# A new order for 1,400 steps: attention with a small state, fused with a snake MLP, on one core

## The chip, the core and the metric

The kernel runs on one core of one Trainium2 chip. A core has five engines with their own instruction queues: TensorE (PE; its weight loads, PEld, are listed apart), VectorE (DVE), ScalarE (ACT), GpSimd (POOL) and SyncE (SP). Sixteen DMA engines move data between the chip's main memory and the core; here SP, ACT and POOL issue transfers. Matmul results are in PSUM, which has eight banks. Each engine does its instructions in order and waits on semaphores for the others.

The metric is the device time of the kernel in microseconds (us). Before the change it is 221.43, the median of three runs (221.27 to 221.89).

## The reference: what is computed

```python
B, H, S, Ns, D = 8, 8, 512, 32, 64
scores = x @ state^T / sqrt(D)          # x: B H S D, state: B H Ns D
xread  = softmax(scores) @ state        # B H S D
scores2 = state @ x^T / sqrt(D)
sread  = softmax(scores2) @ x           # B H Ns D
y = concat([xread, sread], axis=2)      # to rows (B * 544) x 512
h = y @ w_in                            # 512 x 2048
g = h + sin(alpha * h)**2 / (alpha + 1e-9)
out = g @ w_out                         # 2048 x 512, out is 4352 x 512, float32
```

## The kernel before

The product with w_in is moved ahead of the attention's second matmul: for each batch the kernel forms M = state @ w_in once (step `m`), and then h = A @ M, where A holds the softmax weights. So each batch b = 0 to 7 is one tile t of 512 tokens, and the 256 state rows of all batches (32 each) form a ninth tile, t = 8. All matmuls are bf16, accumulated in float32.

There is no loop. The list `ORDER` (from line 21) names every step, with its arguments, in the order in which the program is written; `Steps` has one method for each name, and the last lines run them (lines 629 to 633). Since each engine works in order, this list sets the order of every engine and of every DMA queue. The framework adds the semaphores. Letters A, V, G in a step's arguments put it on ACT, DVE or POOL; a number behind the tile's indices is a PSUM bank, which can be taken only when what was in it has been read.

For a batch b the steps are, in the order in which they depend on each other:

- `lx.b` (line 271): POOL issues the load of x, cast to bf16, into `xnat` (three buffers). Batch 0 comes through `lq`, four float32 loads on SP.
- `pk.b.part` (344): DVE brings half of the heads into the layout `xp`, in which pairs of heads lie side by side. `xq` does it for batch 0.
- `td.b` (387): a DMA transpose, issued by SP, makes `xT` out of `xp`, for batches 2 to 7. Batches 0 and 1 are transposed on TensorE instead (`xtq` 358, `xt` 371) and copied out of PSUM (`xc` 382).
- `sc.b.g` (394): scores for half of the heads; `ex` exponentials on ACT; `rs` and `rr` the row sums and their reciprocals on DVE; `nm` (418) the normalised weights A; `ad.b` (438) a DMA transpose of A into `AT`, issued by SP (batch 0: `at` and `ac`, through TensorE).
- `m.b.s` (478): slice s (512 columns) of M for both halves g, eight matmuls of 64 x 32 weights, which run beside each other in parts of the array; `me` (495) copies a half out of its bank.
- `w`, `cs`, `rc`, `xs` (445 to 474): the second softmax, whose result goes into `xs_all` for tile 8.

For each tile t and each of the sixteen blocks f of 128 hidden columns: `h.t.f` (531) is two matmuls of 512 columns (`hg`, line 549, is one of the two; for t = 8, four of 256); `si` (557) the sine on ACT, `sq` (564) its square on ACT, DVE or POOL, `gt` (573) the sum g on DVE, which frees the bank of h. Then `o.t.st.f0.f1` (581) adds blocks f0 to f1 − 1 into output rows st; `oc` (592) copies the finished bank to `o_sb` (six buffers) on ACT or DVE, and `os` (597) stores it, issued by SP. Tile 7's rows st = 3 are done in two pieces, `oh`, `och`, `osh`, of 384 and 128 columns. The stores of tile 8 are written by line 605, over eight batches of 16 rows:

```python
ov = k.out.rearrange("(b t) c -> b t c", t=k.TB)
k.nc.sync.dma_start(ov[:, k.S + st::2, cols], o_sb[:, cols])
```

The weights are loaded by POOL: `li.s` (280) a slice of w_in, `lo.s` (292) four blocks of w_out, `l_st` the state. Because x comes first and the weights then arrive slice by slice, the front of the list is a race of small steps with these loads; `warm_up.n.cols.bank` (300) gives TensorE n matmuls of zeros whose result nobody reads.

The order at the front of TensorE's queue, from the first product with w_in (steps of other engines left out):

```
at.0.0 warm_up m.0.0 m.1.0 at.0.1 warm_up hg.0.2.0 hg.0.1.0 hg.0.2.1 hg.0.1.1 hg.0.0.0 hg.0.0.1
m.1.1 m.0.1 hg.0.3.0 hg.0.3.1 warm_up m.0.2 m.1.2 hg.0.4.0 hg.0.4.1 ...
```

and at its end, with the copies and stores:

```
o.8.1.11.16 o.8.0.15.16 o.7.0.8.9 oc.8.1.A ... oc.8.0.V o.7.0.10.12 os.8.1 o.7.0.12.13 os.8.0
o.7.0.13.16 o.7.2.0.2 oc.7.0.A o.7.2.2.5 os.7.0 o.7.2.5.11 oh.7.3.0 o.7.2.11.13 och.7.3.0.A
o.7.2.13.15 osh.7.3.0 o.7.2.15.16 oh.7.3.1 oc.7.2.V os.7.2 och.7.3.1.A osh.7.3.1
```

The functions that the diff touches:

## Time and profile before

| what | value |
|---|---|
| median of three runs | 221.43 us |
| the profiled execution | 221.22 us, its span 219.2 us |
| PE busy | 211.4 us, 96% of the span |
| DVE, ACT, POOL busy | 162.9, 173.4, 106.2 us |
| o matmuls (L587) | 542 recorded, 133.9 us |
| h matmuls (L537, L552, L543) | 219, 29 and 64 recorded |
| gt on DVE (L576) | 144, 96.8 us |
| si on ACT (L560) | 144, 88.8 us |
| squares on POOL (L201) | 75, 75.9 us |
| stores, 256 KB each | 33, median 2.3 us from issue to landing |
| loads of x by POOL, 512 KB each | 7, median 7.5 us |
| DMA transposes, xT and AT | 6 and 7, median 4.8 and 3.3 us |

The span is the time from the first to the last instruction on the core; some 2 us of the measured time lie around it. Busy time adds up the durations of instructions. Matmuls overlap: one of 512 columns is listed with about 379 ns, but the next starts 216 ns later, so a busy PE doesn't say how full TensorE is; the spacing of starts does. A few matmul records are missing from the trace. "idle before <- X" is what ended the wait of a group of instructions. A chain of waits is followed backwards from the last instruction. SPq and POOLq are the queues in which those engines issue transfers; such an instruction is short, and the transfer lands later.

### The profile page before, as it was taken

The numbers are of one execution on the slowest core, as the hardware profiler recorded it, in microseconds if no ns is written. First come the engines' busy times: TensorE is split into PE (matmuls) and PEld (weight loads), VectorE is DVE, ScalarE is ACT, GpSimd is POOL, SyncE is SP. The second block draws the span as 40 slices with busy tenths as digits, with TensorE's granted clock in tenths as the row PEclk, the third lists the DMA queues.
The fourth block names the chain that finished last, engine by engine and source line by source line (L and its number), as shares of the span: only waits on it lengthen the run. The fifth ranks groups of instructions, "written<-read, shape, count | busy, mean of one in ns | idle before, by whom it ended". The sixth has DMA issues, their size and how long they took to land.

```text
span 219.2 us, 4303 instructions
## 1 busy us (share of the span) xinstructions
PE 211.4 (96%) x1593; PEld 104.5 (48%) x1619; DVE 162.9 (74%) x287; ACT 173.4 (79%) x297; POOL 106.2 (48%) x114
## 2 busy tenths in 40 slices
PE   7989999999999999999999999999999999999994
PEld 3744544444444534444454444454445555665452
DVE  3769996999787789989888788888667987661201
ACT  4799778997998979898996999798848896785111
POOL 5959533895195647753943387273501082121000
PEclk9999999999999999999999999999999999999999
DMA  6999999987491029167145327470220211012042
GB/s 195 178 206 204 205 204 146 217 169 133 101 238 48 3 92 143 57 144 96 48 79 131 109 71 96 134 110 0 48 100 0 98 48 48 0 51 96 1 143 96
DMA packets 38052, 23.48 MB, mean 107 GB/s; under 512 B 20992, under 2 KB 33680, under 8 KB 38032
## 3 DMA queue, kind: packets, MB, share of 16 engines
q1 hardware_dynamic: 26128, 15.08, 26.5%
q0 software_dynamic: 11648, 8.13, 26.0%
q8 instruction: 12, 0.20, 0.3%
q14 instruction: 8, 0.07, 0.1%
q10 hardware_dynamic: 256, 0.01, 0.1%
HBM read 17.44 MB, written 8.91 MB: 120 GB/s over the span
## 4 chain that ended last, share of the span: by engine, by line
PE 90%; DMA 6%; POOL 1%; issue 1%; ACT 0%
PE o_ps L587 54%; PE h_ps L537 22%; DMA w_in_sb<-in_moe_w_in_dram 5%; PE m_ps L488 4%; PE h_ps L543 3%; PE h_ps L552 2%; PE w_ps L450 2%; PE s_ps L399 2%; PE w_ps L461 1%; DMA s<-in_state_dram 1%; POOL w_in_sb L282 1%; PE x_ps L376 0%; POOL st_nat L267 0%; POOL s01b L255 0%; ACT o_sb L595 0%
## 5 line engine op out<-in xcount | busy, mean ns | idle before, releaser
L587 PE MATMUL o_ps<-w_out_sb,gT 128*128 128x512 bf16 (+2 forms) x542 | 133.9, 373 | 1.6 <-issue 1.0
L576 DVE SCALAR_TENSOR_TENSOR gT<-s,inva_sb,h_ps 128x512 bf16<-128x512 bf16 (+1 forms) x144 | 96.8, 713 | 20.4 <-POOL s L201 10.8
L201 POOL TENSOR_TENSOR s<-s 128x512 bf16<-128x512 bf16 (+1 forms) x75 | 75.9, 1022 | 64.4 <-ACT s L560 62.7
L560 ACT ACTIVATE s<-h_ps,alpha_sb 128x512 bf16<-128x512 f32 (+1 forms) x144 | 88.8, 670 | 11.1 <-PE h_ps L543 4.5
L587 PEld LDWEIGHTS <-gT 128*128 128x128 bf16 x560 | 52.3, 98 | 60.3 <-issue 5.0
L537 PE MATMUL h_ps<-AT,M 128*128 128x512 bf16 x219 | 60.0, 379 | 0.3
L537 PEld LDWEIGHTS <-M 128*128 128x128 bf16 x224 | 21.7, 98 | 25.9 <-issue 0.4
L569 ACT ACTIVATE s<-s 128x512 bf16<-128x512 bf16 (+1 forms) x53 | 31.4, 594 | 0.8
L201 POOL TENSOR_TENSOR A<-E,rR 128x512 bf16<-128x512 bf16 x16 | 16.6, 1056 | 23.8 <-ACT o_sb L595 12.9
L595 ACT COPY o_sb<-o_ps 128x512 f32<-128x512 f32 (+2 forms) x24 | 13.7, 570 | 16.6 <-PE o_ps L587 16.5
L496 ACT CAST M<-m_ps 128x512 bf16<-128x512 f32 x35 | 18.6, 594 | 8.2 <-PE m_ps L488 8.2
L496 DVE CAST M<-m_ps 128x512 bf16<-128x512 f32 x29 | 18.9, 679 | 2.5 <-PE m_ps L488 2.1
L595 DVE COPY o_sb<-o_ps 128x512 f32<-128x512 f32 x11 | 7.5, 685 | 12.9 <-PE o_ps L587 12.9
L201 DVE TENSOR_TENSOR s<-s 128x512 bf16<-128x512 bf16 (+1 forms) x16 | 7.0, 439 | 6.2 <-ACT s L560 6.1
L410 DVE TENSOR_REDUCE R<-E 128x16 f32<-128x512 bf16 x16 | 10.4, 657 | 0.7 <-ACT E L406 0.6
L488 PE MATMUL m_ps<-w_in_sb,stT 64*32 64x512 bf16 x256 | 10.2, 382 | 0.1
L468 DVE RECIPROCAL rC<-w_ps 128x128 f32<-128x128 f32 x8 | 7.6, 948 | 3.3 <-PE w_ps L461 3.2
L303 PE MATMUL warm_ps<-warm 128*128 128x128 bf16 (+3 forms) x66 | 8.6, 271 | 1.4 <-DVE warm L209 1.2
L552 PE MATMUL h_ps<-AT,M 128*128 128x512 bf16 x29 | 8.4, 379 | 0.9 <-ACT M L496 0.7
L406 ACT ACTIVATE E<-s_ps 128x512 bf16<-128x512 f32 x16 | 8.8, 602 | 0.4 <-PE s_ps L399 0.4
L543 PE MATMUL h_ps<-xs_all,w_in_sb 128*128 128x256 bf16 x64 | 9.1, 273 | 0.0
L543 PEld LDWEIGHTS <-w_in_sb 128*128 128x128 bf16 x64 | 6.3, 98 | 3.4
(56 smaller groups left out, 101.8 us busy)
## 6 DMA issues: line engine op xcount, KB each, us to landing
out_dram<-o_sb SPq DMA_DIRECT2D x33, 256.0 KB, 2.3
xnat<-in_x_dram POOLq DMA_DIRECT2D x7, 512.0 KB, 7.5
w_in_sb<-in_moe_w_in_dram POOLq DMA_DIRECT2D x4, 512.0 KB, 10.9
w_out_sb<-in_moe_w_out_dram POOLq DMA_DIRECT2D x4, 512.0 KB, 18.0
x<-in_x_dram SPq DMA_DIRECT2D x4, 256.0 KB, 4.2
st_nat<-in_state_dram POOLq DMA_DIRECT2D x1, 256.0 KB, 5.3
out_dram<-o_sb SPq DMA_DIRECT2D x1, 192.0 KB, 1.9
s<-in_state_dram SPq DMA_DIRECT2D x1, 128.0 KB, 2.2
```

The source lines that it names most:

```text
L201: {"V": k.nc.vector, "G": k.nc.gpsimd}[eng].tensor_tensor(out, a, b, ALU.mult)
L410: k.nc.vector.reduce_sum(R[:, g], k.t["E", b][:, g].rearrange("p c (h j) -> p (c h) j", j=k.Ns), axis=AX.X)
L488: k.nc.tensor.matmul(k.t["m", b, s + n, g][o0:o0 + k.Ns, :], k.stT[k.half(r), b * k.G + g, c0:c0 + k.Ns], k.w_in_sb[k.half(r), 2 * g + h, ...
L496: k.copy(eng)(k.t["M", b][:, g, s * k.FW:(s + 1) * k.FW], k.t["m", b, s, g][:])
L537: k.nc.tensor.matmul(hp[:, :n], k.t["M", t][:, g, fs], k.t["AT", t][:, g, :], start=(g == 0), stop=(g == k.G - 1),)
L543: k.nc.tensor.matmul(hp[:, :n], k.w_in_sb[:, q, fs], k.xs_all[:, q].rearrange("p b j -> p (b j)"), start=(q == 0), stop=(q == k.Q - 1),)
L552: k.nc.tensor.matmul(k.t["h", t, f][:], k.t["M", t][:, g, f * k.P:(f + 1) * k.P], k.t["AT", t][:, g, :], start=(g == 0), stop=(g == k.G - 1),)
L560: k.nc.scalar.activation(s[:, :n], k.t["h", t, f][:, :n], ACT.Sin, scale=k.alpha_sb[:, f:f + 1])
L569: k.nc.scalar.activation(s2[:, :n], s[:, :n], ACT.Square)
L576: k.nc.vector.scalar_tensor_tensor(gT[:, :n], k.t["s2", t, f][:, :n], k.inva_sb[:, f:f + 1], k.t["h", t, f][:, :n], ALU.mult, ALU.add,)
L587: k.nc.tensor.matmul(k.t["o", t, st, half][:, cols], k.t["gT", t, f][:, rows], k.w_out_sb[:, f, cols], start=(f == 0), stop=(f == k.FT - 1),)
L595: k.copy(eng)(o_sb[:, cols], k.t["o", t, st, half][:, cols])
```

## The change

Every step of the list stands in a new place. What is computed, the tiles, their types, the buffers and the count of matmuls for M, h and the outputs stay. These are the differences that are more than order:

- `o` is now one matmul per step, `o.t.st.f`, and may take the blocks f in any order; the bank is taken by a step of its own, `oo`, and the first and last matmul into a bank are found by counting. In the same way `ho` takes the bank of a split h, and `hg` may do its two halves in either order.
- Batch 1's x is transposed on TensorE out of `xp`, two heads (128 columns) at a time, sixteen transposes instead of thirty-two of 64 columns out of `xnat`. `pk.1` therefore comes before it.
- The assignments to engines are others: of 144 squares, ACT has 44 (53 before), DVE 47 (16) and POOL 53 (75); three `nm` go from POOL to DVE, and `me`, `oc`, `xc`, `xq`, `st_c`, `s01_k` change places between ACT and DVE.
- There are five `warm_up` steps, all of 512 columns (16 matmuls), in place of 32 steps of various widths.
- POOL's loads: `li.0` stands ahead of `l_st`; `li.3`, `lo.2` and `lo.3` follow later, among squares; `lx.2`, `lx.3` and `lx.4` follow each other with nothing of POOL's between them; `lx.7` stands ahead of `lx.6`.
- The two halves of the last piece change places, and tile 8's second output, `8.0`, is now the last but one to be finished.

```diff
 ORDER = """
-touch_x l_s01 consts touch lq.0.S ident_ l_alpha lq.1.S zero.0 warm_up.7.512.3 exp_table lq.2.S
-zero.1 identf.V lq.3.S s01_c.G l_st li.0 xq.0.A s01_t.4 li.1 xtq.0.5 warm_up.1.384.3 xq.1.A
...
-o.7.0.8.9 oc.8.1.A o.7.0.9.10 oc.8.0.V o.7.0.10.12 os.8.1 o.7.0.12.13 os.8.0 o.7.0.13.16 o.7.2.0.2.2
-oc.7.0.A o.7.2.2.5 os.7.0 o.7.2.5.11 oh.7.3.0.1 o.7.2.11.13 och.7.3.0.A o.7.2.13.15 osh.7.3.0
-o.7.2.15.16 oh.7.3.1.4 oc.7.2.V os.7.2 och.7.3.1.A osh.7.3.1
+touch_x l_s01 consts touch lq.0.S ident_ l_alpha lq.1.S zero.0 warm_up.5.512.7 exp_table lq.2.S
+zero.1 identf.V lq.3.S s01_c.G ho.0.1.0 s01_t.1 s01_k.1.A s01_k.0.A xq.0.V warm_up.1.512.7 xtq.0.2
+xc.0.0.0.A xq.2.A xq.1.V xq.3.A li.0 l_st warm_up.1.512.7 xtq.1.1 xc.0.0.1.V al_t.2 sc.0.0.1 ex.0.0
+xtq.2.3 xc.0.1.0.V xtq.3.4 xc.0.1.1.A warm_up.3.512.7 sc.0.1.4 ex.0.1 warm_up.6.512.7 m.0.0.4.3
+m.1.0.1.5 rs.0.0 sin_table li.1 li.2 ho.0.0.6 rr.0.0 al_c inva rs.0.1 rr.0.1 me.1.0.0.A nm.0.1.0.4.V
+nm.0.0.0.4.G at.0.0.2 me.0.0.0.V at.0.1.7 st_t.0.1 lo.0 ac.0.0.A hg.0.1.0 ac.0.1.A me.0.0.1.V
+hg.0.1.1 lo.1 me.1.0.1.A si.0.1 ho.0.2.3 st_c.0.1.V ho.0.7.7 st_c.0.0.V hg.0.0.0 hg.0.0.1 hg.0.2.1
+sq.0.1.V gt.0.1 hg.0.2.0 ho.0.3.1 hg.0.3.1 si.0.0 si.0.2 sq.0.0.G hg.0.3.0 m.0.1.5.2 me.0.1.1.V
+me.0.1.0.A si.0.3 gt.0.0 st_t.1.4 st_c.1.0.V st_c.1.1.A m.1.1.0.5 me.1.1.0.A ho.0.4.2 hg.0.4.1
+hg.0.7.1 ho.0.5.6 me.1.1.1.A hg.0.5.0 hg.0.4.0 m.0.2.4.0 si.0.4 hg.0.7.0 sq.0.2.G gt.0.2 me.0.2.1.V
...
+o.0.1.14 oc.0.1.V sq.1.2.V h.1.5.4 si.1.5 h.1.11.7 lx.2.0.1 si.1.11 os.0.1 h.1.12.6
+si.1.12 gt.1.2 h.1.0.3 si.1.0 o.0.3.14 o.0.3.12 o.0.3.11 oc.0.3.A o.0.0.14 lx.3.0.1 lx.4.0.1
+sq.1.11.V gt.1.11 h.1.15.1 si.1.15 o.0.0.13 sq.1.5.G gt.1.5 os.0.3 h.1.13.7 si.1.13 h.1.3.0 si.1.3
+sq.1.12.G o.0.2.15 pk.2.0.V gt.1.12 o.0.2.14 oc.0.2.A sq.1.0.G gt.1.0 pk.2.1.V td.2 sq.1.15.G
...
+o.7.1.12 o.7.1.0 o.8.0.15 o.8.0.12 o.8.1.2 o.7.0.8 oc.7.0.V o.8.0.9 o.7.2.13 o.7.2.1 oc.7.2.V
+o.8.0.3 os.7.0 oh.7.3.1.7 och.7.3.1.V o.8.1.12 o.7.1.13 o.8.1.10 os.7.2 o.8.1.0 o.8.1.6 oc.8.1.V
+o.8.0.13 o.7.1.8 o.7.1.12 o.7.1.11 o.7.1.7 o.7.1.3 oc.7.1.V os.7.1 os.8.1 o.8.0.4 osh.7.3.1 oc.8.0.A
+os.8.0 oh.7.3.0.6 och.7.3.0.A osh.7.3.0
 """.split()
...
         for h in range(2):
             for i in range(k.C):
-                for r in range(2):
-                    k.nc.tensor.transpose(
-                        tp[k.half(r), h, i * k.P:(i + 1) * k.P],
-                        k.t["xnat", b][:, 2 * (2 * g + h) + r, i * k.D:(i + 1) * k.D],
-                        k.ident[:],
-                    )
+                k.nc.tensor.transpose(
+                    tp[:, h, i * k.P:(i + 1) * k.P], k.pair(b, i, 2 * g + h), k.ident[:]
+                )
...
+    def ho(k, t, f, bank):
+        k.t["h", t, f] = k.ps(bank, [k.P, k.S], FP32, "h_ps")
+        k.made["h", t, f] = 0
+
+    def hg(k, t, f, g):
+        k.made["h", t, f] += 1
...
-            start=(g == 0), stop=(g == k.G - 1),
+            start=k.made["h", t, f] == 1, stop=k.made["h", t, f] == k.G,
...
+    def oo(k, t, st, bank, half=None):
+        k.t["o", t, st, half] = k.ps(bank, [k.P, k.DOUT], FP32, "o_ps")
+        k.made["o", t, st, half] = 0
+
+    def o(k, t, st, f, half=None):
...
+        k.made["o", t, st, half] += 1
+        k.nc.tensor.matmul(
+            k.t["o", t, st, half][:, cols], k.t["gT", t, f][:, rows], k.w_out_sb[:, f, cols],
+            start=k.made["o", t, st, half] == 1, stop=k.made["o", t, st, half] == k.FT,
+        )
...
     def oh(k, t, st, half, bank):
-        k.o(t, st, 0, k.FT, bank, half=half)
+        k.oo(t, st, bank, half=half)
+        for f in range(k.FT):
+            k.o(t, st, f, half=half)
```

## The prediction

> **What bounds the kernel now.** I read the page's engine line and chain first, then TensorE's timeline in the first 18 us, then the busy time by stage, then the end.
>
> ```profile
> span 219.2 us, 4303 instructions
> PE 211.4 (96%) x1593; PEld 104.5 (48%) x1619; DVE 162.9 (74%) x287; ACT 173.4 (79%) x297; POOL 106.2 (48%) x114
> PE 90%; DMA 6%; POOL 1%; issue 1%; ACT 0%
> ```
>
> The chain is TensorE for 90% of the span; its DMA part is the load of w_in at the front. So three things can move the end: when TensorE's unbroken stream starts, how long the stream is, and what follows its last matmul. TensorE's timeline (start, us, what):
>
> ```profile
> 11.87 0.63 PE L488 MATMUL m_ps<-w_in_sb,stT 64*32 64x512 bf16 x16
> ...
> 13.78 1.24 PE L552 MATMUL h_ps<-AT,M 128*128 128x512 bf16 x5 [0.73 <-ACT M L496]
> 14.95 0.63 PE L488 MATMUL m_ps<-w_in_sb,stT 64*32 64x512 bf16 x16
> 15.51 0.60 PE L552 MATMUL h_ps<-AT,M 128*128 128x512 bf16 x2
> 16.28 1.05 PE L303 MATMUL warm_ps<-warm 128*128 128x128 bf16 x12 [0.17 <-ACT M L496]
> 17.41 0.62 PE L488 MATMUL m_ps<-w_in_sb,stT 64*32 64x512 bf16 x16
> ```
>
> The three m pairs at 11.87, 14.95 and 17.41 start as slices 0, 1 and 2 of w_in land (11.83, 14.90, 17.37); POOL's loads land one after another, about 2.54 us for each 512 KB. From 17.41 on I added up the order: every 512-wide matmul 0.216 us (the spacing of starts), a group of eight small m matmuls 0.216, entering and leaving a run of small-tile matmuls 0.20. That gives 198.84 us, so an end at 216.25; the last matmul in fact ends at 215.95. There is no stall worth naming after 17.41: this order is full, and a new one can win at most a few tenths per cent at the front.
>
> Stage by stage the other engines have little room:
>
> ```profile
> 37.00:57.00 20.00, 19.74 (x156) 9.23 (x158) 18.06 (x32) 17.82 (x31) 13.62 (x13) 1.00 0.89 159
> 57.00:77.00 20.00, 19.89 (x139) 9.84 (x137) 16.05 (x27) 18.99 (x32) 12.32 (x12) 1.00 0.43 103
> 77.00:97.00 20.00, 19.84 (x133) 8.36 (x133) 18.38 (x33) 17.83 (x31) 12.23 (x13) 1.00 0.57 117
> ```
>
> (PE, PEld, DVE, ACT, POOL.) DVE and ACT are 80 to 95% busy, and DMA 0.89 in the first of these stages. The end, in the timeline and then the landings of the stores issued from 209.6 on:
>
> ```profile
> 207.87 1.49 SPq L605 DMA_DIRECT2D out_dram<-o_sb  x2
> 209.82 6.97 SPq L602 DMA_DIRECT2D out_dram<-o_sb  x4
> 216.15 0.27 ACT L595 COPY o_sb<-o_ps 128x128 f32<-128x128 f32 x1 [1.50 <-PE o_ps L587]
> ```
>
> ```profile
> out_dram<-o_sb SPq DMA_DIRECT2D x2, 256.0 KB, 3.2
> out_dram<-o_sb SPq DMA_DIRECT2D x1, 192.0 KB, 1.9
> out_dram<-o_sb SPq DMA_DIRECT2D x1, 64.0 KB, 1.8
> ```
>
> The two L605 stores (tile 8, the state rows) are unlike the other 33. Their semaphores in the trace get eight late increments each, where an L602 store gets sixteen, and finish at 212.07 and 213.59: 4.2 and 4.8 us after issue, against 2.0 for an ordinary 256 KB store (198.80 to 200.81). os.7.0, issued behind them at 209.82, took 4.4. All that is hidden, because TensorE runs until 215.95. After it: copy, issue at 216.44, landing 218.28, span end 219.21, that is 3.26 us.
>
> **The change, part by part.** The sum is made against the profiled execution (221.22 us: span 219.2 and 2.0 around it); the median of the runs is 0.2 higher.
>
> *Front.* POOL now issues w_in slice 0 before st_nat. Bytes and rate are the same, so slice 0 lands near 10.4, st_nat near 11.8, slices 1 and 2 stay at 14.9 and 17.4. I walked the new order with the row durations (and the spacing of back-to-back instructions: ACT si 0.62, me 0.48; DVE gt 0.67, me 0.60): sc.0.1 at 8.8, exp to 9.85, reduce and reciprocal to 10.7, nm.0.1 on DVE to 11.25, at.0.1 11.3 to 11.7, st_t.0 behind st_nat 11.9 to 12.5, hg.0.1.1 when ac.0.1 ends at 12.8. Eight hg end at 14.6, m.0.1 starts at 14.9 with its slice. m.1.1 waits for bank 5 (me.0.1.0.A, 16.0), four more hg run to 17.23, and m.0.2 waits for bank 0 (me.1.1.0.A, 17.55): 17.60 instead of 17.41. So 0.19 later, but with four more hg behind it. Bounds: 17.41 (the slice) and 18.3 (if ACT and DVE took their full durations with no overlap). A third bound: 512-wide warm-ups stand 0.427 apart until 5.4 and 0.216 after; the new order has fewer fillers, and eight hg at the slow spacing would cost 1.7. I take none of it, since the gaps between the remaining pieces are under 0.7.
>
> *Length of the stream.* From m.0.2: 244 hg and h matmuls instead of 248, and 17 runs of small tiles instead of 18: 197.77 against 198.84, −1.06. Batch 1's transposes are in this: 32 half-width ones took 1.08 with 0.09 before and 0.33 after (25.62 to 27.20, less one matmul); 16 full ones at 0.056 are 0.9 with no such edges. pk.1 must now come before them; DVE reaches it at 25.15 when lx.1 lands, xt.1.1 starts at 25.84 by the walk, against 25.63. The walk arrives at h.1.2 at 36.7 (before 37.0). Front and stream together: +0.19 −1.06 +0.1 of small waits = −0.8. TensorE would end at 215.15.
>
> *Moved loads and stores.* li.3, lo.2 and lo.3 go behind squares on POOL (issued by the walk at 19.7, 24.2 and 26.2). The load pipe is busy until 32.8 either way, so they land at 27.7, 30.2 and 32.8 as before, and are first used at 28.6, 30.9 and 35.0: nothing, with 0.7 us to spare at the least. On SP, os.0.0 goes behind td.4 and ad.3; six o_sb buffers cover it, since oc.2.3, which needs its buffer, comes near 84: nothing.
>
> *Engine shares.* Squares move from POOL (75 to 53) and ACT (53 to 44) to DVE (16 to 47), three nm go from POOL to DVE: DVE gains 31 × 0.44 + 3 × 0.6 = 15.4 us, POOL loses 25, ACT 5. Per 10 us of stream, DVE asks for 0.96, 0.82, 0.97, 0.89, 1.07 of the time in the first five (before: 0.92, 0.79, 0.89, 0.81, 0.80). Where it asks for 1.07 TensorE stalls unless o matmuls are at hand: 0.7 if none are, 0 if enough are.
>
> *Loads of x.* POOL issues lx.2, lx.3 and lx.4 in a row behind sq.0.15, about 35.1 to 37.8, where before they were spread (15.2, 34.0, 43.4). One load alone landed 5.6 after issue, one beside stores 7.3 and 8.2. DVE meets pk.2.0 at 41.0 and pk.3.1 at 44.8, both in front of gt steps whose banks the next h need within 0.3 us; lx.2 lands 40.7 to 42.5, lx.3 43.2 to 45. td.2 then has to land before sc.2.1 (48.8): issued near 43, beside lx.4 and a store, it takes 4.2 (lowest row) to 6.7 (an AT transpose issued with a load, 81.59 to 88.25), so 47.2 to 49.7. Together 0 to 2.5 us of stall. I take 0.7 for this and the DVE stretch, near the low end, because td.2 beside one load took only 5.4. The other td and ad have 1.5 us or more in hand: the tightest, ad.5, lands near 121.7 for an h at 123.1.
>
> *Tail.* Now tile 8 ends last. From the end E of the last matmul back: oh.7.3.0 is 16 × 0.162 = 2.6, o.8.0.4 and o.7.1.3 stand in front. SP has in order os.7.1 (E−1.9, after its DVE copy), os.8.1 (E−1.55), osh.7.3.1 (E−0.7), os.8.0 (E−0.3), osh.7.3.0 (E+0.7, after a 0.48 copy). An ordinary last store would land at E+2.65, 0.32 later than before's E+2.33. But os.8.0 lands, by the row of the pair (first issue to last landing 5.72), at E+4.2, or by its own row (4.83) at E+4.5, with osh.7.3.0 partly behind it. I take E+4.4: +2.1. Low end: packets at their fastest (0.084 each, 16 per engine and store, 1.4 us to the first): E+3.0, +0.7. High end: osh.7.3.0 0.6 behind os.8.0, as os.7.0 was: E+5.0, +2.7.
>
> The Trainium skill ("DMA: Bandwidth & Descriptors", section "Why a DMA increments its semaphore by 16 and not by 1") says that a copy from such a queue runs on the largest count up to 16 that divides the slowest dimension of both sides, which for eight batches of 16 rows is eight engines; the eight increments agree. By that rule alone, an estimate, the 1.0 us of data becomes 2.0 per store, os.8.0 lands at E+3.6 and the sum is 0.8 lower; the rows of the pair are slower than that and I go by them.
>
> Sum: 221.22 − 0.8 + 0.7 + 2.1 = 223.2; against the median, 0.2 higher, **223.4**. The likeliest case's own range is 222.1 to 224.4.
>
> **Rivals.**
> 1. *Faster: the tail costs nothing much.* If the two stores are slow only because of each other and of os.7.0, and SP's small store between them spreads them, the tail is +0.3 and the front stands: 221.4 − 0.8 + 0.3 = 220.9, or 220.5 if m.0.2 starts with its slice and nothing waits until h.1.2. It decides if os.8.0 lands within 2.7 us of its issue; no L605 row is under 4.2. 0.13.
> 2. *No change.* Tail at its low end (+0.7) and no stall: 221.4 ± 0.65. 0.13.
> 3. *Loads and transposes, or DVE, become a bound.* If lx.2 lands at 42.5 or td.2 at 49.7, each tenth goes straight to TensorE: 1.2 to 2.5 more than I take, 224.4 to 225.8. For: DMA is 0.89 busy there already. Against: the three loads are ahead of td.2. 0.19.
> 4. The likeliest as above, 0.55.
>
> **Numbers.** Slower by over 0.3% (0.66 us, about what a measurement of this kernel tells from none): 0.55 + 0.19 = 0.74; same 0.13; faster 0.13. The range 221.0 to 225.3 leaves about 0.1 out on each side.
>
> **What would show it.** Front: an m pair split up, m.0.2 near 17.6, h.1.2 near 36.7. Middle: idle of TensorE at 41 to 50 named by DVE xp or the xT transpose. Tail: last matmul end 1 us or less from 215.6, L605 issues within 2 us of it, last landing over 4 us after it. The prediction is wrong if TensorE's end moves by more than 2 us either way, or if the last store lands within 3 us of the last matmul.

## The result, and the profile after

The changed kernel takes 228.69 us (median of 6 runs, 228.06 to 229.96) against 221.35 us: 1.0337 times the time before, 95% interval 1.0303 to 1.0371. The forecast was 223.4 us, its range up to 225.3. The direction is right and the size is not: 7.3 us lost where 2.0 were expected. The profiled execution took 228.31 us, span 226.5. A run that took over 1.5% longer than the fastest of its kernel is left out of every ratio and interval below, but not out of the medians in us.

The page's head, of the changed kernel:

```profile
span 226.5 us, 4152 instructions
PE 215.0 (95%) x1553; PEld 102.6 (45%) x1553; DVE 183.5 (81%) x323; ACT 171.3 (76%) x286; POOL 82.8 (37%) x89
PE 67%; DVE 16%; ACT 6%; DMA 5%; POOL 2%; issue 2%; SPq 1%; ACTq 0%; POOLq 0%
```

The chain that was TensorE for 90% is now 67% TensorE and 16% DVE: in some stretches TensorE no longer runs through. DVE's busy time rose by 20.6 us where 15.4 had been counted for the work moved to it; the rows below show that instructions there have become longer too.

The busy time by stage (PE, PEld, DVE, ACT, POOL, then granted clock, DMA share, GB/s):

```profile
37.00:57.00 20.00, 17.84 (x107) 7.69 (x106) 18.31 (x29) 15.02 (x25) 14.64 (x15) 1.00 1.04 167
57.00:77.00 20.00, 20.00 (x154) 9.30 (x152) 19.04 (x35) 17.72 (x31) 10.57 (x11) 1.00 0.40 90
77.00:97.00 20.00, 19.52 (x163) 8.71 (x162) 18.06 (x31) 18.78 (x31) 9.81 (x10) 1.00 0.54 110
```

The loss sits in the first stage: PE 17.84 against 19.74 before. The chain of waits of the changed kernel through it (start, us, what):

```profile
34.92 0.65 POOL s L203
35.57 0.54 issue
36.11 6.70 DMA xnat<-in_x_dram
42.81 0.02 issue
42.83 1.25 DVE xp L350
44.08 1.31 DVE gT L578 x2
45.39 0.86 DVE xp L350
46.25 0.66 DVE gT L578
46.91 1.08 DVE s L203
47.99 0.66 DVE gT L578
48.65 0.52 DVE xp L350
49.17 1.99 DVE gT L578 x3
```

lx.2 is issued at 36.11, behind a square on POOL, and lands at 42.81, where 40.7 to 42.5 was forecast. From there the chain is DVE, and four of its pieces are odd: the three copies xp (pk.2.0, pk.2.1, pk.3.1) are listed with 1.25, 0.94 and 0.60 us and the square with 1.16, where such instructions alone take 0.42 (the chain shows a little less of each, because one overlaps the next). td.2 lands at 52.22, 0.49 before sc.2.1 starts, so in this execution it is DVE that sc.2.1 waits for in the end.

TensorE's timeline in the front, of the changed kernel:

```profile
10.18 0.62 PE L487 MATMUL m_ps<-w_in_sb,stT 64*32 64x512 bf16 x16
...
12.28 2.06 PE L554 MATMUL h_ps<-AT,M 128*128 128x512 bf16 x8
...
15.72 1.12 PE L554 MATMUL h_ps<-AT,M 128*128 128x512 bf16 x4
17.21 0.39 PE L487 MATMUL m_ps<-w_in_sb,stT 64*32 64x512 bf16 x2 [0.37 <-ACT stT L342]
17.82 0.40 PE L487 MATMUL m_ps<-w_in_sb,stT 64*32 64x512 bf16 x6 [0.22 <-ACT M L495]
```

The two groups of eight and four hg are there, and m.0.2 comes in two parts, at 17.21 and 17.82, each behind a wait for ACT. The end, in the timeline and then the landings of the stores issued from 213 on:

```profile
219.21 0.78 SPq L609 DMA_DIRECT2D out_dram<-o_sb  x1
220.04 0.40 SPq L606 DMA_DIRECT2D out_dram<-o_sb  x1
220.55 0.66 SPq L609 DMA_DIRECT2D out_dram<-o_sb  x1
220.92 0.48 ACT L599 COPY o_sb<-o_ps 128x384 f32<-128x384 f32 x1 [2.02 <-PE o_ps L591]
221.43 0.39 SPq L606 DMA_DIRECT2D out_dram<-o_sb  x1
```

```profile
out_dram<-o_sb SPq DMA_DIRECT2D x5, 256.0 KB, 2.0
out_dram<-o_sb SPq DMA_DIRECT2D x1, 192.0 KB, 4.2
out_dram<-o_sb SPq DMA_DIRECT2D x1, 64.0 KB, 3.8
```

The tile 8 stores (L609) are issued at 219.21 and 220.55; SP's waits for them end at 223.66 and 225.14, 4.5 and 4.6 us later. The 192 KB store behind them takes 4.2 and is the last to land, at 225.61.

To place the loss I cut every profile at three marks: the first h matmul of tile 1 (h.1.2), the first score matmul of batch 2 (sc.2.1), and the end of the last matmul. "Middle" is from the first mark to the second, "rest" from the second to the third, "tail" from there to the end of the span. Before: h.1.2 at 36.96, middle 12.09, rest 167.07, tail 3.09. After: 37.50, 15.21, 168.18, 5.66. So 0.5 + 3.1 + 1.1 + 2.6 = 7.3 of span; the time of the two executions differs by 7.1, since 2.0 us lie around the span before and 1.8 after. (By the records the last matmul before ends at 216.12; the prediction had read 215.95.)

### The profile page after: what moved, and what is told of

The parts are those of the page before. It is cut to its first block, busy times and chain, and to the rows that moved or that the text cites. A ratio compares the mean times of both kernels' runs of the same rounds, so it can differ in the third digit from the quotient of the medians.

```text
span 226.5 us, 4152 instructions
## 1 busy us (share of the span) xinstructions
PE 215.0 (95%) x1553; PEld 102.6 (45%) x1553; DVE 183.5 (81%) x323; ACT 171.3 (76%) x286; POOL 82.8 (37%) x89
## 4 chain that ended last, share of the span: by engine, by line
PE 67%; DVE 16%; ACT 6%; DMA 5%; POOL 2%; issue 2%; SPq 1%; ACTq 0%; POOLq 0%
PE o_ps L591 41%; PE h_ps L536 16%; DVE gT L578 7%; PE h_ps L542 3%; DMA xnat<-in_x_dram 3%; PE m_ps L487 3%; DVE xp L350 3%; ACT s L562 2%; DVE s L203 2%; DMA x<-in_x_dram 2%; POOL s L203 2%; ACT M L495 2%; PE w_ps L449 1%; PE s_ps L398 1%; DVE M L495 1%
## 5 line engine op out<-in xcount | busy, mean ns | idle before, releaser
L591 PE MATMUL o_ps<-w_out_sb,gT 128*128 128x512 bf16 (+2 forms) x560 | 140.2, 373 | 0.1
L203 POOL TENSOR_TENSOR s<-s 128x512 bf16<-128x512 bf16 (+1 forms) x53 | 55.1, 1050 | 102.9 <-ACT s L562 76.7
L536 PE MATMUL h_ps<-AT,M 128*128 128x512 bf16 x224 | 63.1, 379 | 2.7 <-DVE gT L578 2.6
L571 ACT ACTIVATE s<-s 128x512 bf16<-128x512 bf16 (+1 forms) x44 | 25.8, 590 | 1.0
L203 DVE TENSOR_TENSOR s<-s 128x512 bf16<-128x512 bf16 (+1 forms) x47 | 21.6, 462 | 2.6 <-ACT s L562 2.2
L599 ACT COPY o_sb<-o_ps 128x512 f32<-128x512 f32 (+1 forms) x21 | 12.3, 584 | 11.4 <-PE o_ps L591 11.4
L203 POOL TENSOR_TENSOR A<-E,rR 128x512 bf16<-128x512 bf16 x13 | 13.9, 1076 | 17.2 <-DVE rR L415 6.6
L599 DVE COPY o_sb<-o_ps 128x512 f32<-128x512 f32 (+1 forms) x14 | 9.2, 660 | 7.3 <-PE o_ps L591 7.2
L350 DVE COPY xp<-xnat 128x1024 bf16<-128x1024 bf16 x14 | 10.0, 721 | 0.6 <-DMA xnat<-in_x_dram 0.5
L554 PE MATMUL h_ps<-AT,M 128*128 128x512 bf16 x32 | 8.8, 380 | 0.0
L398 PEld LDWEIGHTS <-xT 128*128 128x128 bf16 x128 | 5.8, 98 | 4.1 <-issue 1.1
```

What stands on the lines that cost most here:

```text
L203: {"V": k.nc.vector, "G": k.nc.gpsimd}[eng].tensor_tensor(out, a, b, ALU.mult)
L350: k.copy(eng)(k.t["xp", b][:, :, hs, :], k.t["xnat", b][:, hs, :].rearrange("p h (i d) -> p i h d", i=k.C),)
L536: k.nc.tensor.matmul(hp[:, :n], k.t["M", t][:, g, fs], k.t["AT", t][:, g, :], start=(g == 0), stop=(g == k.G - 1),)
L571: k.nc.scalar.activation(s2[:, :n], s[:, :n], ACT.Square)
L591: k.nc.tensor.matmul(k.t["o", t, st, half][:, cols], k.t["gT", t, f][:, rows], k.w_out_sb[:, f, cols], start=k.made["o", t, st, half] == 1 ...
L599: k.copy(eng)(o_sb[:, cols], k.t["o", t, st, half][:, cols])
```

## The experiments

All are edits of the changed kernel, except two that edit the kernel before. One caution for reading them: the front of the changed order varies from execution to execution. Over the eleven profiles in which nothing of it is edited the first m matmul starts between 10.18 and 12.21, and everything shifts with it, so the stretches say more than the totals.

**1. Three suspects, one at a time.** Issue lx.2 early (behind lo.3); leave out tile 1's POOL squares; or compute them and let nobody read them.

```
  lo.3 lx.2.0.1 nm.1.0.0.4.G ...            # a: lx.2 moved up

  def sq(k, t, f, eng):                      # b: no squares on POOL in tile 1
+     if t == 1 and eng == "G":
+         k.t["s2", t, f] = k.t["s", t, f]
+         return

      k.mul(eng, s2[:, :n], s[:, :n], s[:, :n])   # b2: computed, not read
+     if t == 1 and eng == "G":
+         k.t["s2", t, f] = s
```

> The changed kernel with one step moved: lx.2 (batch 2's x) is issued right behind lo.3, near 26, instead of behind sq.0.15 at 36.1, so that it no longer shares the queue with lx.3 and lx.4. Loads theory (late x is what stops the middle): lx.2 lands near 34, pk.2.0 can run near 41.5 and td.2 goes out some 2 us earlier, so most of the 3.1 us that TensorE lost between 37.5 and 52.7 comes back: 225.7 to 226.4 against 228.7. Port theory (DVE's copies and squares wait out POOL's squares): only DVE's 0.53 us of idle time for lx.2 can come back, and pk.2.0 still takes 0.9 us or more wherever it meets a square: 227.9 to 228.4.

> The changed kernel without tile 1's squares on POOL: that tile's gate takes the sine itself in place of its square wherever POOL squared it (part of the computation is left out). The squares on DVE and ACT stay. Port theory: pk.2.0, pk.3.1 and pk.3.0 fall from 1.25, 0.94 and 0.60 us to 0.42, tile 1's DVE squares from about 0.67 to 0.40, and of the 3.1 us that TensorE lost between 37.5 and 52.7 less than 1 is left: 225.8 to 226.9 against 228.7. Loads theory: DVE still reaches pk.2.0 before lx.2 has landed (42.8) and td.2 goes out no earlier, so little changes: 228.0 to 228.7.

> As the kernel without tile 1's POOL squares, but POOL still computes them and nobody reads them (that tile's gate takes the sine itself there, so part of the computation is left out). It takes away only the wait of a gate for POOL's result and leaves POOL's work beside DVE's. Port theory: pk.2.0 and pk.3.1 keep 0.9 us or more and TensorE still loses 2 us or more between 37.5 and 52.7: 227.6 to 228.7. Rival (the gates were late because POOL's squares came late, not because the two engines exclude each other): as without the squares, 225.8 to 226.9.

Measured: 229.12, 230.49 and 231.22 us; middle 13.65, 14.37 and 15.21. No one expectation held. (The copies that the expectations call pk.3.1 and pk.3.0 are pk.2.1 and pk.3.1.) Without the squares the copies did fall to 0.43, 0.42, 0.43 us, as the port theory said, and with squares that nobody reads they stayed at 1.23, 0.94, 0.60, and the middle at 15.21: DVE is held by POOL's work, not by POOL's results. But the time did not come back, because td.2 took the place of DVE as the limit: it landed at 53.53, 1.78 after lx.4, and sc.2.1 started at 53.58. With lx.2 early the middle lost 1.6 us less, but ad.1, the AT transpose that h.1.2 waits for, was now behind lx.2: issued at 34.30, it landed at 40.11, 1.0 after lx.2 (in the changed kernel 33.18 to 36.32), and h.1.2 started at 40.15. The two kernels without these squares in the gates' way were slower in total, by 0.9 and 1.6 us against the changed kernel's second set of runs, which was on the same chip (229.6 us without the run of 233.24). I can follow that only in part: the rest was 0.7 and 1.2 longer in their profiles, 0.6 and 0.7 of it in one wait near 72.6 behind a DVE square that took 1.20 and 1.24 us, and the front of the first was 1.7 later, which its edit doesn't touch.

**2. The changed kernel again, lx.4 after td.2, and both.**

```
- sq.0.15.G ... lx.2.0.1 ... lx.3.0.1 lx.4.0.1 ...
+ sq.0.15.G ... lx.2.0.1 ... lx.3.0.1 ... sq.1.8.G lx.4.0.1 ...
```

> The changed kernel unchanged, for a second profile of it and times from the same chip as the three runs beside it. All theories: 228.1 to 229.5; of the profile, the middle (first h of tile 1 to the first score matmul of batch 2) again 15.2 us, the tail after TensorE again 5.6. What may move is the front: the first slice of w_in landed at 9.46 in the first profile and between 9.86 and 11.39 in four kernels with the same front.

> The changed kernel with one step moved: lx.4 is issued behind sq.1.8.G (near 47.7) instead of at 37.9, so it is no longer in front of td.2 in the load pipe. Two limits in parallel (DVE, which loses time to POOL's squares, and td.2, which in every profile so far lands 1.8 to 1.95 us after lx.4): td.2 lands near 50.6 instead of 52.2, but DVE's chain is as late as before, so the middle stays at 14.9 to 15.2 us and the time within 0.4 of the changed kernel's. Loads theory alone: the middle falls to 13.1 or less, 2 us off the time.

> Both at once: lx.4 behind the place of sq.1.8.G, and tile 1's squares left out on POOL (its gate takes the sine there, so part of the computation is left out). Two limits in parallel: now neither stands, the middle falls from 15.2 us to 12.1 to 12.9, against 14.4 without the squares alone and about 15 with lx.4 moved alone: 2.3 to 3.1 off the changed kernel's time. Rival (something else holds the middle, such as lx.3 for pk.3.1): 13.7 or more.

Measured: the changed kernel again 1.0321 times before (1.0239 to 1.0404), middle 14.83, rest 168.17, tail 5.66, first m matmul 12.21. With lx.4 late the middle fell to 13.66, between the two expectations, and td.2 landed at 50.01. That is not the loads alone: td.2 was there 1.36 us before sc.2.1 and held nothing, but DVE's chain had become shorter too, with the copy pk.2.0 at 0.48 (before 1.25), the square at 0.60 (1.16) and the wait for lx.2 at 0.30 (0.53). lx.2 had landed 5.09 us after h.1.2 instead of 5.31, and in all twelve profiles with these squares POOL starts one 5.26 after h.1.2: where pk.2.0 starts 4.72 to 5.22 after h.1.2 it ends at 5.58 to 5.65, and where it starts at 5.33 to 5.37 it ends at 6.58, just behind that square. In the repeat, and in three kernels of sections 4 and 5, lx.2 landed 4.8 to 5.2 after h.1.2 as well, with lx.4 in its place, and there td.2 held the middle at 14.3 to 15.0. So two limits in parallel stand; only my "DVE's chain is as late as before" failed. The time was 1.0326 times before (1.0240 to 1.0412), not to be told from the changed kernel's, with rest 168.89. The third kernel did not do what its text says: with the squares gone POOL had nothing to wait for in front of lx.4 and issued it at 38.63 all the same; it is a second run of the kernel without squares (middle 15.51, 230.04 us).

So the squares were cut to 8 columns, which keeps POOL's place in time:

```
+     if t == 1 and eng == "G":
+         n, k.t["s2", t, f] = 8, s
      k.mul(eng, s2[:, :n], s[:, :n], s[:, :n])
```

> lx.4 issued behind sq.1.8.G, and tile 1's squares on POOL cut to 8 of 512 columns (and not read: its gate takes the sine there, so part of the computation is left out). So POOL keeps its place in time, unlike in the kernel without these squares, where POOL had nothing left to wait for and issued lx.4 at 38.6 in spite of the new order. With lx.4 moved alone the middle was 13.7 us, without the squares alone 14.4 and 15.5, in the changed kernel 15.2 and 14.8. Theory (DVE shut out by POOL, and the x loads in front of td.2, are two limits of which one always stands): with both gone the middle is 12.1 to 12.9. Rival (lx.2 and lx.3 landing late, which this leaves as it is): 13.5 or more.

Measured: 1.0350 times before (1.0298 to 1.0402), middle 15.34: the rival. The copies took 0.43, 0.42, 0.43 us, but DVE sat 0.91 us for lx.2 and 1.19 us for lx.3 (issued 38.90, landed 49.54), and td.2 took 7.8 us and landed 0.04 before sc.2.1. Why td.2 took that long here and 4.5 with lx.4 late alone, no run settles.

**3. The loads back to the start.** The changed order issues lo.0 at 10.09 and lx.1, li.3, lo.2, lo.3 behind squares; the kernel before had lo.0 out at 6.31. The windows of the two kernels, first before, then after (the last column is GB/s, the one ahead of it the DMA share):

```profile
24.00:28.00 4.00, 3.84 (x57) 2.35 (x57) 3.40 (x8) 3.51 (x6) 1.04 (x1) 1.00 1.24 204
28.00:32.00 4.00, 4.00 (x36) 1.65 (x36) 3.84 (x8) 2.90 (x4) 1.04 (x2) 1.00 1.28 203
32.00:36.00 4.00, 3.95 (x19) 1.86 (x19) 2.19 (x4) 3.45 (x7) 2.91 (x4) 1.00 1.16 165
36.00:40.00 4.00, 4.00 (x21) 1.77 (x19) 3.50 (x7) 3.54 (x7) 0.99 (x1) 1.00 1.47 159
```

```profile
24.00:28.00 4.00, 3.74 (x37) 2.14 (x36) 3.54 (x6) 2.36 (x4) 2.96 (x4) 1.00 1.01 160
28.00:32.00 4.00, 3.96 (x42) 1.70 (x39) 3.81 (x9) 3.94 (x7) 0.49 (x1) 1.00 1.14 165
32.00:36.00 4.00, 4.00 (x21) 1.75 (x18) 3.87 (x7) 3.90 (x6) 1.63 (x2) 1.00 0.55 101
36.00:40.00 4.00, 4.00 (x20) 1.83 (x19) 3.06 (x6) 2.11 (x5) 3.26 (x5) 1.00 0.62 72
```

From 24 on the load pipe runs partly dry, and at 32 to 40 it moves 101 and 72 GB/s where it moved 165 and 159 before, while the loads of x still have to come. Three kernels: only the issues moved; that and tile 8's steps first (see 4); that and tile 1's squares cut to 8 columns.

```
+ lo.0 lo.1 lx.1.0.1 nm.0.0.0.4.G li.3 lo.2 lo.3 lx.2.0.1 ...   # and nowhere else
```

> The changed kernel with POOL's load issues put back to the start: lo.0, lo.1 and lx.1 in front of batch 0's first normalisation, li.3, lo.2, lo.3 and lx.2 right behind it (near 6.4 to 13 instead of 10.1 to 36.1). Nothing else moves. Dry-pipe theory: the pipe runs through, lx.2 lands near 35.4 and not 42.8 to 44.2, lx.3 near 43.5, td.2 goes out near 43.5 and lands by 49; the middle falls from 15 us to 12.1 to 13.3, and with lo.2 and lo.3 in time the front by up to 0.3: 1.8 to 3.2 off the changed kernel's 228.7 to 229.7. Rival (DVE's exclusion by POOL still holds the middle): 14.5 or more stays, at most 0.8 off.

> The early load issues and tile 8's steps first, together. If the two causes are separate they add: 1.9 from the tail (measured alone: 5.66 to 3.72) and what the early loads alone give beside it; by the dry-pipe theory 223.9 to 225.4. By the rival 226.5 to 227.4.

> As early loads with tile 8 first, and tile 1's squares on POOL cut to 8 of 512 columns and not read (part of the computation is left out). It shows what DVE's exclusion is worth when the loads are in time: with the loads late the squares' removal moved the middle from 15.2 to between 14.4 and 15.5. If exclusion is then the next limit, the middle goes to 12.1 to 12.3, 0.5 to 1.2 less than in the same kernel with the squares; if it has slack everywhere in the middle, no change from that kernel.

Measured: 228.24, 226.34 and 225.32 us (1.0316, 1.0220 and 1.0180 times before; 1.0303 to 1.0330, 1.0198 to 1.0242, 1.0166 to 1.0194); middle 13.65, 13.65 and 12.09. The first middle lies between its two expectations, as does the second total. lx.2 landed at 34.82, 35.29 and 34.64 as it was said to, and the pipe moved 206 and 202 GB/s at 24 to 32. In the first kernel the total fell by only 0.4 to 1.4, less than the 1.8 to 3.2 expected; its profiled execution had a late front (first m matmul 11.76, h.1.2 at 38.90), which took back what the middle gave. What is left of the middle's loss there is DVE alone. Its five instructions that meet a POOL square, in the second kernel:

```profile
41.56 0.79 DVE L205 TENSOR_TENSOR s<-s 128x512 bf16<-128x512 bf16 x1
43.71 0.86 DVE L352 COPY xp<-xnat 128x1024 bf16<-128x1024 bf16 x1
45.81 0.94 DVE L352 COPY xp<-xnat 128x1024 bf16<-128x1024 bf16 x1
47.33 0.60 DVE L205 TENSOR_TENSOR s<-s 128x512 bf16<-128x512 bf16 x1
48.51 0.60 DVE L352 COPY xp<-xnat 128x1024 bf16<-128x1024 bf16 x1
```

From 39.84 on DVE goes from one instruction to the next without a wait, for a load or for a result of POOL. With the squares cut to 8 columns the same five take 0.42 each. The four combinations of the middle, one line each:

```
squares whole,  loads late    15.21  14.83  15.21  15.21  15.21  15.01  14.71  14.27
squares gone,   loads late    14.37  15.51  15.34
squares whole,  loads early   13.65  13.65
squares gone,   loads early   12.09                (before: 12.09)
```

(In the first line stand all kernels whose edits lie outside the middle, and the one with unread squares; the kernels with only lx.2 early or only lx.4 late had 13.65 and 13.66.) What held the middle, for each group: its loss against 12.09, DVE's waits for x in it, by how much its copies and squares took longer than 0.42 in all, and how long before sc.2.1 td.2 had landed:

```
                                                 loss           wait         longer        td.2 ahead
changed, more fillers, tile 8 first, unread sq.  3.12           0.53 to 0.56 2.6           0.14 to 0.49
lx.2 early; lx.4 late; loads early (two)         1.56 to 1.57   0 to 0.30    1.3 to 1.7    1.2 to 1.5
loads early and squares cut (two)                0.00           0            0.0           0.2
changed again, fewer fillers, both layouts       2.18 to 2.92   0.09 to 1.36 1.2 to 2.1    0.04 to 0.05
squares gone or cut, loads late (three)          2.28 to 3.42   0.95 to 2.83 0.0           0.04 to 0.05
```

That settles the middle. In the first three groups DVE's waits and its longer instructions add up to the loss within 0.15, and td.2 has time in hand; in the last two td.2 lands last, 1.7 to 2.0 us after lx.4 in all of them but the kernel with lx.4 late and squares of 8 columns. So there are two limits, and only with both gone does TensorE run as before. In the changed kernel's first profile POOL's squares stretch DVE by 2.6 and lx.2 makes it wait 0.53. Part of the 2.6 is lx.2's doing: it landed 5.31 after h.1.2, and so its copy waited out the square that begins at 5.26. With lx.2 early that copy starts 4.72 after h.1.2 and the loss is 1.56, which ends with the squares. With the loads late, taking the squares away gave nothing that stands out of the scatter, since td.2 then held.

**4. The tail.** Twice I gave tile 8's rows the order row-then-batch, so that the slowest dimension of its stores is 16 and not 8: once by writing xs_all in that order, once by reading it so. A third kernel keeps the stores and moves tile 8's last o matmuls, copies and stores ahead of all else behind the last gate.

```
- ov = k.out.rearrange("(b t) c -> b t c", t=k.TB)
- k.nc.sync.dma_start(ov[:, k.S + st::2, cols], o_sb[:, cols])
+ n = k.Ns // 2
+ ov = k.out.rearrange("(b t) c -> t b c", t=k.TB)
+ k.nc.sync.dma_start(ov[k.S + st * n:k.S + (st + 1) * n, :, cols], o_sb[:, cols])

- k.xs_all[k.half(r), :, b, :]                               # first: written in the new order
+ k.xs_all[k.half(r), :, :, b]
- k.xs_all[:, q].rearrange("p b j -> p (b j)")               # second: read in the new order
+ k.xs_all[:, q].rearrange("p b j -> p j b")

  gt.8.3 <all o.8, oc.8, os.8 that are left> <the rest, as it was>   # third
```

> The changed kernel with tile 8's 128 rows in the order row-then-batch, so that its two stores have a slowest dimension of 16 (rows) and not of 8 (batches); the same bytes, the same runs of 512 bytes, the same steps. Tail theory (eight engines carry the two stores, and they end last): each store gets sixteen increments, lands within 2.5 us of its issue, and the end is again a small store some 3.3 us after the last matmul in place of 5.8: 226.1 to 226.8 against 228.7. Rival (the stores are slow because of their order on the queue and of each other): they still take 4 us or more, 228.3 to 229.0.

> Tile 8's rows in row-then-batch order as in the first store experiment, but xs_all is written as in the changed kernel and TensorE reads it in the new order (64 matmuls of tile 8 with a strided moving operand). Tail theory: the two stores land about 3.0 us after issue and the time from the last matmul to the end falls from 5.66 to 4.1: 1.5 off the time if the strided read costs TensorE nothing. Rival: the strided read slows the 64 matmuls (0.273 us each); at twice the time it costs 9 us.

> The changed kernel with the last steps in another order: after the last gate, tile 8's remaining o matmuls, copies and stores come first, and the rest in its old order. The same instructions. Tail theory: the tile 8 stores are issued 4 us or more before TensorE ends and are hidden, the last store is an ordinary small one, and the time after the last matmul falls from 5.66 to 3.1 to 3.5: 2.2 to 2.5 off the changed kernel's 228.7 to 229.7. Rival (the tail is long because four stores crowd into the last 2.5 us, whichever they are): 4.1 or more stays, at most 1.5 off.

Measured: 232.38 us (1.0495 times before, 1.0446 to 1.0545), 1.127 times before (1.1175 to 1.1365), and 227.40 us (1.0269, 1.0232 to 1.0307); tail 4.13, 4.10 and 3.72. The first two totals say nothing of the tail, since each layout cost more than it gave. The groups of the tile xs_all, in the changed kernel, with the strided write, and with the strided read (ns min/median/max; its granted clock was 0.953 on the mean, but 1.00 at 182 to 190, where the first eight of the 64 took 0.589 to 0.609):

```profile
L542 PE MATMUL h_ps<-xs_all,w_in_sb x64: 272/273/273, 181.1 to 206.8; 128*128 128x256 bf16 x64
L470 DVE TENSOR_TENSOR xs_all<-w_ps,rC x16: 273/286/295, 59.5 to 173.6; 64x128 bf16<-64x128 f32 x16
```

```profile
L470 DVE TENSOR_TENSOR xs_all<-w_ps,rC x16: 712/725/943, 59.4 to 178.8; 64x128 bf16<-64x128 f32 x16
```

```profile
L542 PE MATMUL h_ps<-xs_all,w_in_sb x64: 588/607/617, 181.8 to 233.3; 128*128 128x256 bf16 x64
```

The tails themselves are as expected: with sixteen rows outermost the two stores land 3.00 and 3.04 us after issue instead of 4.5 and 4.6. So of the 2.57 us that the tail grew, 1.5 go with the eight engines; the other 1.0 is left for four stores in the last 2.5 us, which is what remains and was not measured apart. With tile 8 first the tail is 3.72, 1.94 less, a little above my 3.1 to 3.5: the last store is issued behind a copy of 0.48 (before 0.27) and lands 2.26 after issue (before 1.84).

**5. The front and the two small terms.** Seven more fillers in the first 8.8 us; the nine 512-wide fillers in front of m.0.0 cut to three; batch 1's packed transposes alone in the kernel before; slice 0 of w_in ahead of the state rows alone in the kernel before.

```
+ warm_up.1.384.7 xtq.0.2 ... warm_up.2.448.7 xtq.1.1 ... warm_up.1.384.7 sc.0.0.1 ...   # f
+ ... warm_up.1.256.7 xtq.2.3 ... warm_up.2.128.7 xtq.3.4 ...
- warm_up.3.512.7 sc.0.1.4 ex.0.1 warm_up.6.512.7                                        # n
+ warm_up.1.512.7 sc.0.1.4 ex.0.1 warm_up.2.512.7
- pk.1.0.V hg.0.10.1 xt.1.1.6 pk.1.1.V          # g, with the new body of xt
+ pk.1.1.V hg.0.10.1 xt.1.1.6 pk.1.0.V
- l_st li.0                                      # l
+ li.0 l_st
```

> The changed kernel with seven more filler matmuls between the first transposes and score matmuls of batch 0 (before 8.8 us), about as the kernel before has them. Clock theory: in the second profile TensorE was busy only 1.16 of 2 us at 4 to 6, its granted clock fell to 0.50 at 8 to 10, and the first m matmul came at 12.21 instead of 10.18; with fillers the clock stays at 1.00 and the first m matmul comes at 10.2 to 11.2, and the runs lie at 228.0 to 228.6 with less spread. Rival (the late quarter of x alone sets it): no change, 228.1 to 230.

> The changed kernel with the nine 512-wide fillers in front of the first m matmul cut to three. Filler theory (they stand between the last score matmul of batch 0 and m.0.0 and run at the slow spacing in some executions): m.0.0 begins with the landing of slice 0, 9.5 to 11, and the runs lie 0.3 to 1.2 lower than the changed kernel's 228.1 to 230.0. Rival (the fillers keep the clock up, or what stands before them is late): no change, or up to 1 us slower because the m and hg matmuls after 10 us run at the slow spacing.

> The kernel before with only batch 1's x transposed packed at full width: 16 matmuls of 128x128 in place of 32 half-wide ones, the two pk.1 copies in the other order, nothing else moved. By the prediction's terms (0.9 in place of 1.08 + 0.09 + 0.33, and up to 0.2 later start behind pk.1.1): 0.3 to 0.6 faster, 220.9 to 221.1 against 221.4. Rival: the start of the transposes moves later by as much as the packing saves: no change.

> The kernel before with only the first two loads on POOL's queue swapped: slice 0 of w_in ahead of the state rows, as in the changed kernel. By the prediction's terms (same bytes and rate) slices 1 and 2 land as before, and m.0.2 still starts with slice 2 at 17.4: no change, 221.0 to 221.8. Rival (the swap is why slice 2 landed at 15.8 in the changed kernel's first profile): m.0.2 up to 1 us earlier, 220.3 to 220.8.

Measured: 229.44 us (1.0361, 1.0316 to 1.0405); 228.57 us (1.0368, 1.0301 to 1.0434); 1.0029 (1.0000 to 1.0058); 1.0185 (1.0145 to 1.0225).

Two windows of the second profile of the changed kernel are why the fillers were tried:

```profile
4.00:6.00 2.00, 1.16 (x10) 0.38 (x6) 0.43 (x1) 1.32 (x3) 2.00 (x4) 1.00 1.03 301
8.00:10.00 2.00, 2.00 (x15) 1.29 (x13) 1.30 (x4) 1.38 (x3) 0.00 (x0) 0.50 1.16 204
```

A quarter of x was late, TensorE idled for 1.24 us in one piece before 6.72, the granted clock fell to 0.50, and m.0.0 came at 12.21, 2.2 after its slice. With fillers the clock stayed at 1.00 and m.0.0 came at 10.91; with few, it began with its slice, at 10.25. Neither made the kernel faster than the spread of its front. What else sets that spread is left open. The Trainium skill ("TensorE: Matmul & The Clock Gate", section "Part 1: The HAM clock gate (the "warmup" mystery)") says that the clock is gated by TensorE's activity in a free-running window, so that the same kernel runs a different number of slow matmuls from one execution to the next. The rows agree that the number differs: the three fillers in front of sc.0.1 took 0.81 us in the first profile (7.72) and 1.49 in the second (8.84). That a window is the reason no run here shows; TensorE also had less to do in the second, because x was late.

The packed transposes alone give nothing, where I had them at 0.3 to 0.6: sixteen full ones take 1.07 us in the trace (32 half-wide ones took 1.08), and the next o matmul, whose record seems to be missing from the trace before, follows 0.1 sooner at most; the score matmuls behind then wait for the evacuation. Swapping the first two loads alone costs 3.3 us, for in the old order 32 transposes of the state rows stand in front of m.0.0. The state rows now land at 11.66 instead of 8.66, TensorE waits 2.86 us for them, the granted clock is 0.50 at 12 to 14, and m.0.0 starts at 15.83. It tells nothing of the new order, which has m.0.0 ahead of them, except that the two edits belong together.

**6. What is left after 52 us.** All POOL squares from tile 1 on cut to 8 columns, with early loads and tile 8 first.

> Early loads and tile 8 first, and all of POOL's squares from tile 1 on cut to 8 of 512 columns and not read (part of the computation is left out). Exclusion theory for the later stalls (0.73 at 96 behind a DVE square of 1.28 us, 0.39 at 118 behind a copy of 1.29 us): both vanish, TensorE's time from the first score matmul of batch 2 to its last matmul falls from 168.2 (168.9 with only tile 1's squares cut) to 167.1 to 167.5, and the time to 223.2 to 224.2. Rival (the later stalls belong to the new order itself, to gates or transposes): 168.2 or more stays, 225.0 to 225.8.

Measured: 223.49 us (1.0091, 1.0074 to 1.0108), middle 12.09, rest 166.75, tail 3.72: as expected, the rest a little better. The DVE groups, first the copies before, after and with the squares cut in tile 1, then DVE's squares after and with all POOL squares cut:

```profile
L348 DVE COPY xp<-xnat x14: 408/419/588, 25.1 to 139.8; 128x1024 bf16<-128x1024 bf16 x14
```

```profile
L350 DVE COPY xp<-xnat x14: 412/598/1286, 25.2 to 118.7; 128x1024 bf16<-128x1024 bf16 x14
L203 DVE TENSOR_TENSOR s<-s x47: 284/419/1276, 13.7 to 203.6; 128x512 bf16<-128x512 bf16 x43, 128x256 bf16<-128x256 bf16 x4
```

```profile
L352 DVE COPY xp<-xnat x14: 415/418/1290, 26.1 to 117.1; 128x1024 bf16<-128x1024 bf16 x14
```

```profile
L205 DVE TENSOR_TENSOR s<-s x47: 284/419/436, 15.6 to 201.5; 128x512 bf16<-128x512 bf16 x43, 128x256 bf16<-128x256 bf16 x4
```

The medians show little of it; the maxima are what to read. In the changed kernel nine of the fourteen copies and ten of the 47 squares run beside a POOL square, with means of 0.89 and 0.67 us against 0.42 and 0.40 alone. The two later stalls are the same thing: 0.73 at 96.14, right after a DVE square of 1.28 at 94.97, and 0.39 at 118.2 behind a copy of 1.29. With POOL's squares cut both are gone. The scatter of the rest is of the same kind: in five of the kernels above with 168.8 to 169.4 a DVE square takes 1.20 to 1.26 near 67.6 to 70.7, which it doesn't in the changed kernel (0.58 at 68.69).

No version here beats the kernel before; the best one that computes everything, early loads and tile 8 first, is 1.022 times its time (1.0198 to 1.0242).

## Why the prediction was right, and where it was wrong

Against the profiled execution the forecast was 223.2 and it took 228.3. By the marks above: h.1.2 0.8 later than I had it, TensorE from there to its last matmul 4.1 longer (183.4 against 179.3), tail 0.5 longer; 5.4 of span, of which the shorter time around the span takes back 0.2. Of the 4.1, 2.4 lie in the middle, 1.1 in the rest, and 0.5 is a shorter stream that didn't come. The step that failed is the one on the engine shares: DVE's copies and squares were left at the durations that they have alone.

*Engine shares and the DVE stretch: the step that failed.* I gave each square moved to DVE 0.44 us and left the copies as they were, from rows in which POOL rarely ran beside them; that DVE and POOL could wait for each other was not in it. The trace before had the sign: three of its copies met a POOL square, and the longest took 0.588. In the changed kernel POOL has fewer squares, 53 for 75, but they fall beside DVE's copies and squares, and in the middle they stretch DVE by 2.6 us, where 0.7 was taken for this and the loads together. In the rest it is the two stalls of 0.73 and 0.39, where nothing was forecast; with the squares cut the rest is 1.4 shorter, 0.3 of it not placed. The Trainium skill ("SBUF — State Buffer", section "Who interferes with whom") says that DVE and GpSimd share a port pair under an exclusive lock, which a copy in a fast mode or an instruction with two SBUF inputs has to wait for until the other's instruction ends. The rows agree: copies and squares take up to 0.87 us longer beside squares of about 1.04; the gates, with one input in PSUM, do not (maximum 0.749, as before). That the port is the reason is the skill's word; the runs show that POOL's squares are.

*Loads of x: the place right, the part of it small.* The place (41 to 50 us) and lx.2, pk.2.0, pk.3.1 and td.2 were as named, with pk.2.1 between them. lx.2 at 42.81 was 0.3 past its window, which cost 0.53 and the meeting with POOL's square at 5.26 after h.1.2; lx.3 at 47.96 was 3 us past, td.2 at 52.22 2.5 past. My rows had a load alone or beside stores; three behind one another took 6.7, 10.9 and 12.4. td.2 had 0.49 in hand in the first profile and 0.04 in the second, so it is the next limit and in some executions the first. This is rival 3, near the top of its price in the middle (0.7 and 1.2 to 2.5 more, against 3.1); it had nothing for the rest.

*Moved loads: the landings wrong, the cost of nothing right.* "The load pipe is busy until 32.8 either way, so they land at 27.7, 30.2 and 32.8 as before." The issue times were right (19.93, 24.30, 26.47 against 19.7, 24.2, 26.2), the conclusion was not: they landed at 27.68, 31.63 and 34.91, 7 us or more after issue, since a pipe that is fed one load at a time, behind squares, runs dry. But TensorE's waits in this trace have no load of weights among those that ended them.

*Tail: right in mechanism, near in size.* Tile 8's second store landed 4.2 us after the last matmul (4.4 taken), the 192 KB store behind it 0.5 later, near the high end that I gave. The tail grew by 2.6, inside my 0.7 to 2.7 and above the 2.1 taken. The pair's own rows were the better price: my estimate by the Trainium skill's rule of the largest divisor ("DMA: Bandwidth & Descriptors", section "Why a DMA increments its semaphore by 16 and not by 1") had eight engines cost 1.0 us more per store; the runs with sixteen show 1.5.

*Front: 0.8 late.* m.0.2 waited for ACT twice (I had walked only the second wait, for bank 0) and was complete 0.2 later than I had it. xt.1.0 lost 0.42 waiting for pk.1.0, a copy of 1.26 us beside a POOL square: the same missing term. The packing was counted in this stretch at 0.6 (1.08 + 0.09 + 0.33 against 0.9), and alone it gave nothing: 11.33 us from the first transpose to h.1.2 before, 11.31 with it. These don't add up to 0.8 exactly, and the remainder is not placed. Of the slow spacing I took none because "the gaps between the remaining pieces are under 0.7". In the second profile there was a gap of 1.24 and a slow stretch behind it, but it fell on the fillers; the eight hg took 2.08 us there and 2.06 in the first.

*Length of the stream: half.* With every stall gone the changed order needs 178.84 us from h.1.2 to its last matmul, before 179.16: 0.3 saved, 0.5 forecast. The missing 0.2 is not placed; the packing lies ahead of h.1.2.

*os.0.0, td and ad later on: nothing, as said*; behind 57 us no stall but the two of section 6 is above 0.15. The rival "the tail costs nothing" fell on every profile, and "no change" with it. The two conditions under which I called the forecast wrong were written down, and one was met: TensorE's end moved by 4.8 us.

## What to carry to other kernels

Moving work from one engine to another is not priced by its duration alone: look at what the two engines do to each other at the same time, and read the maxima of the groups beside the medians. A queue of loads that runs ahead of its readers is slack for everything behind it; when its issues are put behind other work, price the last load of the row, not the first. And when one suspected cause is taken away and nothing happens, that is no acquittal: try it together with the second, as the middle here needed both. When a time does fall, read the chain again before the edit gets the credit: with lx.4 late the middle fell by 1.5, and by the rows it needed lx.2 to land 0.2 us earlier as well, which the edit was not made for.

## What was not expected of the hardware

- A DVE copy of 128x1024 bf16 takes 0.42 us alone and up to 1.29 beside a POOL square; a DVE square of 128x512 bf16 0.40 and up to 1.28.
- A DVE product of 64x128 written with a stride of 8 elements takes 0.725 us instead of 0.286; a 256-wide matmul whose moving operand is read with a stride of 32 elements 0.607 instead of 0.273.
- An idle stretch of 1.24 us of TensorE before 6.72 was followed by a granted clock of 0.50 at 8 to 10, and in the kernel without tile 1's POOL squares one of 0.76 before 5.18 as well. In another execution three 512-wide fillers at 8.14 took 1.49 us (0.43 apiece) while the granted clock read 1.00.
- td.2, issued while lx.3 and lx.4 were in the pipe, landed 1.7 to 2.0 us after lx.4 in the ten profiles that have this order of loads, 5.9 to 7.8 us from issue, where most later ones take about 3.1 (AT) or 4.4 (xT).
